# Two batches in two waves of 256 tokens instead of one after the other, at the start of a fused attention and FFN kernel

## The chip, the cores and the metric

The kernel runs on one core of a Trainium2 chip. The metric is device time in microseconds (us); 371.22 us is the median of three runs of the kernel before, which lie between 371.21 and 371.28. The span of a profile, from the first instruction to the last, is a little shorter than the time of the same execution.

## The reference

Block-causal attention over 8 batches, 8 heads, 576 tokens and a head dimension of 64, then a gated FFN on all 4608 tokens of 512 features:

```python
def _attn_ref(q, k, v):                      # [8, 8, 576, 64] each, f32
    scores = scale * np.matmul(q, k.transpose(0, 1, 3, 2))
    mask = (pos[:, None] // 64) >= (pos[None, :] // 64)     # blocks of 64
    scores = np.where(mask, scores, -1000000000.0)
    ...                                      # softmax over the last axis
    return np.matmul(attn, v)

x = attn_out.transpose(0, 2, 1, 3).reshape(B * S, H * D)    # [4608, 512]
gate = np.maximum(x @ w_gate, 0.0)           # w_gate, w_val: [512, 1536]
out = (gate * (x @ w_val)) @ w_out           # w_out: [1536, 512]
```

## The kernel before, in words

Matmuls run in bf16, with sums in f32. The first 512 tokens of a batch are an *FFN tile*; the last 64 tokens of all eight batches (the *tails*) form the ninth. Heads are handled in pairs, `hp`, and `r = 4 * b + hp` numbers the 32 pairs of all batches.

For a pair, `scores` (matmul L418) computes scores transposed, keys on the partitions, in blocks of 128 tokens. Its two heads lie on partitions 0 to 63 and 64 to 127, so that their matmuls use two halves of the array. `exp` (L428, ScalarE, ACT) writes exponentials to `attnT[r % 2]`. A 128 by 128 block on the diagonal has one 64 by 64 corner that the mask forbids; `corners` (L498, L499) sets it to zero. `head_av` (L564) multiplies by v with a column of ones beside it, so that column 64 holds the sum. `normalise` (L511, L512, VectorE, DVE) divides and writes `xnat`, which `to_xT_pe` (L609) transposes on TensorE (PE) into `xT`, copied out of PSUM at L613 to L616. With 512 tokens a head has 10 blocks of scores at or below the diagonal.

q, k and v of the first batches come through `Early`: a DMA from the SP queue into an f32 tile `stage` (10 buffers), a cast to bf16 on POOL (GpSimd; L215 for q and k, L245 for v), then transposes on PE (`pe_mains`, L313) with copies out of PSUM (L316) into `qTm` and `kTm`. q and k have four consecutive tokens on a partition, so that a run of DRAM is 1 KB; the copies put them back in order. In batch 0, v is loaded with one token on a partition (`load_v`, runs of 256 bytes) and cast straight to `v_bf` (L231). In batch 1, v is loaded packed like q and k, cast to `v_p`, and brought into order by matmuls with a 0/1 matrix `sel` (`sort_v`, L263), in four groups of 32 rows, with the copies at L272.

The FFN is a generator, `ffn_gen`. An FFN *unit* is one of 12 columns of 128 hidden features: four matmuls for the gate and four for the value (L656), a Relu on ACT (L665) and a product on DVE to `hT` (L669). Then come four output blocks of 12 matmuls each (L677), copied at L687 and stored. `ffn(n)` lets it run on by n matmuls, to the end of a unit or block. PSUM has 8 banks: `take(1)` and `pair()` hand out banks 0 to 5, those taken longest ago first; banks 6 and 7 (`AV`) are for attention times v.

Every engine runs its instructions in the order in which the code issues them. The order at the start is written by hand: batch 0's loads, casts and attention first, with the weights' loads and casts (L407) behind, then FFN tile 0, in which `ffn(...)` calls alternate with the attention of batch 1. The end of tile 0 also has the transposes (`pe_tails`, L336) and scores of the tails (`scores_last`, L470; `scores_tails`). Tile 1 needs `xT` of batch 1. Where a few matmuls (`junk`, L716) multiply zeros, they only keep PE busy.

Of the kernel before, what the change touches and what calls it, by code (L numbers as in the profile page):

```python
# [17 lines left out]
def kernel(  # L18
# [23 lines left out]

    consts = ctx.enter_context(tc.tile_pool(name="consts", bufs=1))
# [5 lines left out]
    AV = 6  # L49
# [33 lines left out]
    zeros = consts.tile([128, 512], BF, name="zeros")  # L83
    nc.vector.memset(zeros, 0.0)

    sel = consts.tile([128, 516], BF, name="sel")
# [13 lines left out]
    def selection(eng):  # L100
        eng.memset(sel, 0.0)
        for c in range(4):
            ps = slice(32 * c, 32 * c + 32)
            eng.tensor_copy(
                sel[ps].rearrange("p (j m) -> p j m", j=4)[:, :, 0:128:4],
                ident[ps, None, 32 * c : 32 * c + 32].to_broadcast([32, 4, 32]),
            )
# [35 lines left out]
    class Early:  # L143
# [10 lines left out]

        def load(self, st, src, h0, n, eng=None):
            (eng or nc.sync).dma_start(  # L156
                st.rearrange("p (h n) -> p h n", h=n),
                src[self.b, h0 : h0 + n, 0:512, :].rearrange(
                    "h (p j) d -> p h (j d)", j=4
                ),  # L160
            )
# [13 lines left out]

        def load_v(self, h0, n):
            st = self.st[2, h0] = new_stage(256 * n)
            for h in range(n):
                nc.sync.dma_start(
                    st[:, 256 * h : 256 * h + 256].rearrange("p (c d) -> p c d", c=4),  # L180
                    v[self.b, h0 + h, 0:512, :].rearrange("(c p) d -> p c d", p=128),
                )
# [47 lines left out]
        def cast_v(self, h0, n, eng):  # L230
            eng(  # L231
                v_bf[self.b % 2][:, 0:4, h0 : h0 + n, 0:64].rearrange(
                    "p c h d -> p h c d"
                ),
                self.st[2, h0].rearrange("p (h c d) -> p h c d", h=n, c=4),
            )

# [18 lines left out]
        def sort_v(self, h0, engs):  # L256


            tp = [pair() for _ in range(2)]
            for j in range(4):  # L260
                for c in range(4):
                    ps = slice(32 * c, 32 * c + 32)
                    nc.tensor.matmul(  # L263
                        tp[c // 2][:, c % 2, 0:256],
                        sel[ps, 128 * j : 128 * j + 128],
                        v_p[ps, j, 64 * h0 : 64 * h0 + 256],
                        start=(j == 0),
                        stop=(j == 3),
                        skip_group_check=True,
                    )  # L270
            for i in range(2):
                engs[i](  # L272
                    v_bf[self.b % 2][:, 2 * i : 2 * i + 2, h0 : h0 + 4, 0:64],
                    tp[i][:, :, 0:256].rearrange("p g (h d) -> p g h d", d=64),
                )
# [134 lines left out]
    def scores(b, hp, sc, pieces):  # L410
        for pos, c, main in pieces:
            for hh in range(2):
# [3 lines left out]
                if main:  # L416
# [3 lines left out]
                    kTm[b % 2][ps, c, hp, :],  # L420
# [9 lines left out]
    def scores_1(r):  # L430

        b, hp = divmod(r, 4)
        at = attnT[r % 2]
        sc = scores(b, hp, banks[:, 0:2] if r % 2 == 0 else banks[:, 2:4], [(0, 0, True)])
        exp(at[:, :, 0:512], sc)
        sc = scores(
            b, hp, banks[:, 2:4] if r % 2 == 0 else banks[:, 0:2],
            [(0, 1, True), (384, 3, True)],
        )
        exp(at[:, :, 512:1024], sc)  # L440

    def scores_2(r):
        b, hp = divmod(r, 4)
        sc = scores(b, hp, banks[:, 0:2] if r % 2 == 0 else banks[:, 2:4], [(0, 2, True)])
# [499 lines left out]
```

## Time and profile before

| | |
|---|---|
| median of the runs | 371.22 us |
| profiled execution: its time, its span | 371.53 us, 369.7 us |
| PE busy | 355.9 us, 96% of the span |
| DVE, ACT, POOL busy | 163.2, 172.3, 116.5 us |
| first scores on PE | 6.48 us from the span's start |
| first FFN matmul of tile 0 | 20.34 us |
| first FFN matmul of tile 1 | 66.41 us |
| granted TensorE clock | 1.0 throughout |

A timeline row gives the start, the time that it covers, the engine, line and operation, output and inputs with their shapes, a count, and in brackets the idle time ahead of it on that engine with what ended it. PEld is the loading of weights into the array, which overlaps PE. SPq and ACTq rows are the issues of DMAs. Matmuls overlap each other, so PE's step from one group to the next is the difference of their starts, not the time of a row.

### The profile page before, as it was taken

How to read it: one execution, taken by the hardware profiler on the slowest of the kernel's cores; microseconds unless marked ns; L12 is line 12 of the kernel's file. 1: busy time of each engine (PE TensorE's matmuls, PEld its weight loads, DVE VectorE, ACT ScalarE, POOL GpSimd, SP SyncE). 2: the span in 40 equal slices, each digit the busy share in tenths (PEclk: the TensorE clock that was granted, in tenths of full speed). 3: DMA queues.
4: the chain of work that ended last, by engine and by line, in shares of the span. 5: the costliest groups of instructions: out<-in, count | busy, mean ns of one | idle time of the engine just before them, and what ended most of it. 6: DMA issues, size and time to landing. Idle time of an engine off the chain costs nothing.

```text
span 369.7 us, 7494 instructions
## 1 busy us (share of the span) xinstructions
PE 355.9 (96%) x2961; PEld 187.3 (51%) x3000; DVE 163.2 (44%) x319; ACT 172.3 (47%) x271; POOL 116.5 (31%) x163
## 2 busy tenths in 40 slices
PE   6799899999999999999999999999999999999995
PEld 3545356555555555555555555555555544444443
DVE  4634345376375543444434443444344434423422
ACT  5934656756574563465435543644364403302310
POOL 8677775156778404900391013000000000000000
PEclk9999999999999999999999999999999999999999
DMA  8999989779999979997499829072200130020013
GB/s 255 291 370 355 376 181 328 153 177 256 196 164 167 153 126 94 181 82 151 82 181 92 139 76 136 19 140 68 92 16 18 47 101 0 2 85 29 2 42 100
DMA packets 140227, 51.02 MB, mean 138 GB/s; under 512 B 119584, under 2 KB 133152, under 8 KB 140192
## 3 DMA queue, kind: packets, MB, share of 16 engines
q1 hardware_dynamic: 78528, 34.29, 39.8%
q0 software_dynamic: 56384, 7.08, 35.8%
q10 hardware_dynamic: 5280, 9.18, 7.0%
q8 instruction: 23, 0.38, 0.5%
q14 instruction: 12, 0.10, 0.1%
HBM read 37.75 MB, written 9.44 MB: 128 GB/s over the span
## 4 chain that ended last, share of the span: by engine, by line
PE 85%; DMA 9%; DVE 1%; ACT 1%; issue 1%; POOL 1%; SPq 1%; DVEq 0%; POOLq 0%
PE banks L656 46%; PE banks L677 24%; PE banks L564 7%; PE banks L418 6%; DMA stage<-in_moe_w_gate_dram 3%; DMA stage<-in_v_dram 2%; DMA qTt<-q_bt 2%; DMA stage<-in_k_dram 1%; PE banks L530 1%; SPq L156 1%; ACT attnT L428 0%; DVE hT L669 0%; ACT xT L616 0%; PE banks L609 0%; POOL v_p L245 0%
## 5 line engine op out<-in xcount | busy, mean ns | idle before, releaser
L428 ACT ACTIVATE attnT<-banks 128x1024 bf16<-128x1024 f32 (+1 forms) x124 | 89.8, 811 | 60.4 <-PE banks L418 59.7
L665 ACT ACTIVATE gate_sb<-banks 128x512 bf16<-128x512 f32 x108 | 65.2, 603 | 100.9 <-PE banks L656 100.6
L669 DVE TENSOR_TENSOR hT<-gate_sb,banks 128x512 bf16<-128x512 bf16 x108 | 74.2, 687 | 83.7 <-PE banks L656 74.1
L656 PE MATMUL banks<-xT,wg 128*128 128x512 bf16 x366 | 98.0, 379 | 1.0
L656 PE MATMUL banks<-xT,wv 128*128 128x512 bf16 x378 | 98.4, 379 | 0.3
L677 PE MATMUL banks<-wo,hT 128*128 128x512 bf16 (+1 forms) x432 | 96.1, 373 | 0.6
L656 PEld LDWEIGHTS <-wv 128*128 128x128 bf16 x432 | 42.3, 98 | 51.0
L677 PEld LDWEIGHTS <-hT 128*128 128x128 bf16 x444 | 42.3, 98 | 46.1
L656 PEld LDWEIGHTS <-wg 128*128 128x128 bf16 x432 | 40.4, 98 | 45.9 <-issue 0.8
L687 DVE COPY ob<-banks 128x512 f32<-128x512 f32 (+1 forms) x37 | 25.1, 677 | 54.0 <-PE banks L677 53.2
L361 POOL DMA_DIRECT2D v_bf<-in_v_dram x16 | 14.1, 901 | 70.1 <-PE banks L564 68.1
L564 PE MATMUL banks<-v_bf,attnT 128*128 128x65 bf16 x832 | 35.1, 194 | 1.0 <-POOL v_bf L231 0.6
L564 PEld LDWEIGHTS <-attnT 128*128 128x128 bf16 x832 | 30.6, 98 | 9.7 <-issue 1.6
L418 PE MATMUL banks<-qTm,kTm 64*128 64x512 bf16 (+3 forms) x256 | 25.0, 298 | 2.4 <-ACT attnT L428 1.4
L512 DVE TENSOR_TENSOR xnat<-banks,recip 128x640 bf16<-128x640 f32 (+2 forms) x36 | 25.9, 721 | 1.2
L418 PEld LDWEIGHTS <-kTm 64*128 64x128 bf16 x512 | 17.1, 94 | 12.4 <-issue 3.1
L511 DVE RECIPROCAL recip<-banks 128x10 f32<-128x10 f32 (+3 forms) x38 | 8.0, 210 | 30.3 <-PE banks L564 28.5
L498 DVE MEMSET attnT<- 64x192 uint32 x28 | 6.1, 218 | 23.1 <-ACT attnT L428 20.3
L361 POOL DMA_DIRECT2D q_bf<-in_q_dram x16 | 14.4, 941 | 0.0
L361 POOL DMA_DIRECT2D k_bf<-in_k_dram x16 | 14.2, 928 | 0.7 <-DMA v_bf<-in_v_dram 0.6
L656 PE MATMUL banks<-xTt,wg 128*128 128x512 bf16 x48 | 12.3, 379 | 0.1
L656 PE MATMUL banks<-xTt,wv 128*128 128x512 bf16 x46 | 12.1, 379 | 0.1
(90 smaller groups left out, 194.5 us busy)
## 6 DMA issues: line engine op xcount, KB each, us to landing
out_dram<-ob ACTq DMA_DIRECT2D x32, 256.0 KB, 2.3
stage<-in_moe_w_gate_dram SPq DMA_DIRECT2D x6, 512.0 KB, 9.4
stage<-in_moe_w_val_dram SPq DMA_DIRECT2D x6, 512.0 KB, 9.6
stage<-in_q_dram SPq DMA_DIRECT2D x6, 512.0 KB, 6.4
stage<-in_k_dram SPq DMA_DIRECT2D x6, 512.0 KB, 7.6
stage<-in_moe_w_out_dram SPq DMA_DIRECT2D x6, 512.0 KB, 9.0
stage<-in_v_dram SPq DMA_DIRECT2D x8, 256.0 KB, 6.4
q_bf<-in_q_dram POOLq DMA_DIRECT2D x16, 128.0 KB, 5.9
```

Source lines behind the costliest of these rows:

```text
L361: nc.gpsimd.dma_start(dst, src[b, :, 128 * c : 128 * c + n, :].rearrange("h p d -> p h d"),)
L418: nc.tensor.matmul(o, kTm[b % 2][ps, c, hp, :], qTm[b % 2][ps, c:4, hp, :] if main else qTt[b % 2][ps, hp, :], start=True, stop=True,)
L428: nc.scalar.activation(out, sc, AF.Exp, scale=scale)
L498: eng.memset(three[:, :, :, 0:64], 0.0)
L511: nc.vector.reciprocal(recip, av[:, :, :, 64])
L512: nc.vector.tensor_tensor(out=out, in0=av[:, :, :, 0:64], in1=recip.to_broadcast([rows, heads, n, 64]), op=AX.mult,)
L564: nc.tensor.matmul(av[:, 0, p, :], w, vb[:, c, h, :], start=(p == 0), stop=(c == p), skip_group_check=True,)
L656: nc.tensor.matmul(out[:, t, :], (wg, wv)[t][i][:, c, fo : fo + 128], x[:, c, :], start=(c == 0), stop=(c == 3),)
L665: nc.scalar.activation(gate_sb, out[:, 0, :], AF.Relu)
L669: nc.vector.tensor_tensor(out=h, in0=gate_sb, in1=out[:, 1, :], op=AX.mult)
L677: nc.tensor.matmul(op, hT[f][:, 128 * s : 128 * (s + 1)], wo[f // 4][:, f % 4, n0:n1], start=(f == 0), stop=(f == 11),)
L687: nc.vector.tensor_copy(ob, op)
```

## The change

`Early(0)` and `Early(1)` no longer stand for batches 0 and 1, but for two *waves*: wave 0 has tokens 0 to 255 of both batches, wave 1 tokens 256 to 511 of both. The first half of the partitions holds batch 0 and the second half batch 1. Each wave is an FFN tile, and the stores go to the rows that fit. Wave 0 needs 3 blocks of scores per head and batch (`scores_a`, `av_a`); wave 1 needs 7 (`scores_b`, `av_b`, once per pair and batch), with keys from both waves. Loads of q, k and v become two DMAs of 64 partitions each. v of wave 0 is packed and sorted by matmuls too; `sort_v` now uses two groups of 64 rows. The first FFN units of tiles 0 and 1 are merged, so that their matmuls go by the four head pairs: the last pair's `xT` is read by the last four of 16 matmuls.

```diff
+    def chunk(b, c):
+        return (c // 2, 2 * b + c % 2) if b < 2 else (b % 2, c)
...
+            self.parts = (
+                [(0, b, 0, 512)]
+                if b > 1
+                else [(64 * i, i, 256 * b, 256) for i in range(2)]
+            )
         def load(self, st, src, h0, n, eng=None):
+            for p0, b, s0, ns in self.parts:
+                (eng or nc.sync).dma_start(
+                    st[p0 : p0 + ns // 4].rearrange("p (h n) -> p h n", h=n),
+                    src[b, h0 : h0 + n, s0 : s0 + ns, :].rearrange(
+                        "h (p j) d -> p h (j d)", j=4
+                    ),
+                )
...
+        def sort_v(self, h0, engs, out=None):
+            out = pair() if out is None else out
+            for odd in range(2):
+                for j in range(4):
+                    for g in range(2):
+                        ps = slice(64 * g, 64 * g + 64)
+                        nc.tensor.matmul(
+                            out[:, g, 256 * odd : 256 * odd + 256],
+                            sel[ps, odd, 128 * j : 128 * j + 128],
+                            v_p[ps, j, 64 * h0 : 64 * h0 + 256],
...
+    def scores_a(hp):
+        at = wave_a(hp)
+        sc = banks[:, 0:2]
+        scores_wave(hp, sc, [(0, 0, 0, 0, 2), (256, 0, 2, 2, 2)])
+        exp(at[:, :, 0:512], sc)
+        sc = banks[:, 2:4]
+        scores_wave(hp, sc, [(0, 0, 1, 1, 1), (128, 0, 3, 3, 1)])
+        exp(at[:, :, 512:768], sc[:, :, 0:256])
...
+    def scores_b(hp, b):
+        at = attnT[b]
+        sc = pair()
+        scores_wave(hp, sc, [(256 * c, 0, 2 * b + c, 4 + 2 * b, 2) for c in range(2)])
+        exp(at[:, :, 0:512], sc)
+        sc = pair()
+        scores_wave(
+            hp, sc,
+            [(0, 1, 2 * b, 4 + 2 * b, 2), (256, 1, 2 * b + 1, 4 + 2 * b + 1, 1)],
+        )
+        exp(at[:, :, 512:896], sc[:, :, 0:384])
...
+            groups = [(0, 1)] if j < 2 else [(0,), (1,)]
+            groups += [(f,) for f in range(2, 12)]
...
-        for h0 in (2, 4, 6):
-            e0.load_qk(h0, 2)
-        for h0 in (0, 2, 4, 6):
-            e0.load_v(h0, 2)
+        e0.load_qk(2, 2, nc.scalar)
+        e0.load_v_packed(0)
+        e0.load_qk(4, 2)
+        e0.load_qk(6, 2)
+        e0.load_v_packed(4)
...
+        scores_a(0)
+        e0.pe_mains(1, (dve, dve), banks[:, 4:6])
+        scores_a(1)
+        e0.cast_qk(4, 2, (pool, pool))
+        corners_a(0, nc.gpsimd)
+        e0.sort_v(0, (dve, dve), banks[:, 6:8])
+        e0.cast_qk(6, 2, (pool, pool))
+        corners_a(1, nc.gpsimd)
+        e0.cast_v_packed(4, pool)
+        e0.pe_mains(2, (dve, act), banks[:, 4:6])
+        av_a(0, banks[:, 6:8])
+        scores_a(2)
+        corners_a(2, nc.gpsimd)
+        e0.pe_mains(3, (dve, dve), banks[:, 4:6])
+        av_a(1, banks[:, 6:8])
+        scores_a(3)
+        e0.sort_v(4, (act, dve), banks[:, 4:6])
+        corners_a(3, nc.vector)
         cast_w(w_0[0], pool)
+        to_xT_pe(0, (act,), banks[:, 0])
+        av_a(2, banks[:, 6:8])
+        to_xT_pe(1, (act,), banks[:, 1])
+        av_a(3, banks[:, 4:6])
         cast_w(w_0[1], pool)
+        to_xT_pe(2, (act,), banks[:, 2])
+        to_xT_pe(3, (act, dve), banks[:, 3])
...
+        ffn(40)
         e1.pe_mains(0, (dve, act))
         ffn(8)
+        scores_b(0, 0)
+        corners_b(0, nc.vector)
+        e1.pe_mains(1, (dve, act))
+        ffn(8)
+        scores_b(0, 1)
+        corners_b(1, nc.vector)
         e1.sort_v(0, (dve, act))
         ffn(8)
+        av_b(0, 0)
+        scores_b(1, 0)
+        corners_b(0, nc.vector)
+        av_b(0, 1)
+        wave_to_xnat(4, banks[:, AV : AV + 2])
+        scores_b(1, 1)
+        corners_b(1, nc.vector)
+        ffn(12)
...
+        scores_b(3, 0)
+        corners_b(0, nc.vector)
+        av_b(2, 1)
+        wave_to_xnat(6, banks[:, AV : AV + 2])
         e0.pe_tails((dve, act))
+        scores_b(3, 1)
+        corners_b(1, nc.vector)
+        e1.pe_tails((dve, act))
         to_xT_pe(6, (act,))
         scores_last(0)
+        av_b(3, 0)
+        scores_tails(0)
+        av_b(3, 1)
+        wave_to_xnat(7, banks[:, AV : AV + 2])
+        scores_last(1)
         to_xT_pe(7, (dve,))
```

POOL, from its first q cast on, in the kernel before (`v_bf` is written straight from `stage`):

```order
L215 CAST q_bf<-stage 128x2x4x64
L215 CAST k_bf<-stage 128x2x4x64
L215 CAST q_bf<-stage 128x2x4x64
L215 CAST k_bf<-stage 128x2x4x64
L215 CAST q_bf<-stage 128x2x4x64
L215 CAST k_bf<-stage 128x2x4x64
L498 MEMSET attnT_91 64x2x3x64
L499 MEMSET attnT_91 64x2x64
L231 CAST v_bf_93<-stage 128x2x4x64
```

and the same place after the change, where `v_p` is the packed v:

```order
L223 CAST q_bf<-stage 128x2x4x64
L223 CAST k_bf<-stage 128x2x4x64
L245 CAST v_p<-stage 128x4x4x64
L223 CAST q_bf<-stage 128x2x4x64
L223 CAST k_bf<-stage 128x2x4x64
L462 MEMSET attnT_91 64x2x3x64
L463 MEMSET attnT_91 64x2x64
L223 CAST q_bf<-stage 128x2x4x64
L223 CAST k_bf<-stage 128x2x4x64
```

The cast of v for heads 0 to 3 has moved ahead of q and k of heads 4 to 7, and the zeroing of the first pair's corners ahead of heads 6 and 7.

DVE at the end of tile 0 before (`ob` is an output block, L512 normalises the last pair, `qTt` are the tails' q of the two batches):

```order
L687 COPY ob<-banks 128x512
L511 RECIPROCAL recip<-banks 128x2x4
L512 TENSOR_TENSOR xnat<-banks,recip 128x2x4x64
L337 COPY qTt_83<-banks 128x256
L337 COPY qTt_84<-banks 128x256
L616 COPY xT<-banks 128x512
```

and after (L480 is `corners_b`, which can only run when the exponentials of its batch and pair are written; L583 normalises):

```order
L752 COPY ob<-banks 128x512
L480 MEMSET attnT_91 64x2x2x32
L582 RECIPROCAL recip<-banks 128x2x4
L583 TENSOR_TENSOR xnat<-banks,recip 128x2x4x64
L338 COPY qTt_83<-banks 128x256
L480 MEMSET attnT_92 64x2x2x32
L338 COPY qTt_84<-banks 128x256
L582 RECIPROCAL recip<-banks 128x2x4
L583 TENSOR_TENSOR xnat<-banks,recip 128x2x4x64
L675 COPY xT<-banks 128x512
```

Two zeroings and one more normalisation now stand between the last output block and the last copy to `xT`.

More of the change, by code (lines that the diff above doesn't have):

```diff
@@ L254, in cast_v_tail @@
                 eng(v_diag(self.b % 2, hh), self.st["t", 2][64 * hh : 64 * hh + 64])
[L256 to L270, printed above, removed]
+        def sort_v(self, h0, engs, out=None):
[8 more added lines that the diff above has]
+                            v_p[ps, j, 64 * h0 : 64 * h0 + 256],
+                            start=(j == 0 and odd == 0),
+                            stop=(j == 3),
+                            skip_group_check=True,
+                        )
             for i in range(2):
@@ new lines, in av_b @@
+    def av_b(hp, b, heads=(0, 1)):
+        at = attnT[b]
+        for hh in heads:
+            av = banks[:, AV + hh, 0:260].rearrange("p (n d) -> p n d", d=65)
+            for i in range(2):
+                for c in range(3 + i):
+                    k_i, k_c = chunk(b, c)
+                    col = 768 if c == 3 else 256 * c + 128 * i
+                    nc.tensor.matmul(
+                        av[:, 2 * b + i, :],
+                        at[:, hh, col : col + 128],
+                        v_bf[k_i][:, k_c, 2 * hp + hh, :],
+                        start=(b == 0 and i == 0 and c == 0),
+                        stop=(c == 2 + i),
+                        skip_group_check=True,
+                    )
@@ L554, in head_av @@
         vb = v_bf[b % 2]
[L555 to L557 removed]
+        av = banks[:, AV + hh, 0:325].rearrange("p (n d) -> p n d", d=65)
+        for p in range(NCH):
             for c in range(p + 1):
```

243 lines of the change are left out of this document (104 added, 139 removed).

## The prediction

> **What bounds the kernel now.** I read the page first, then the stages, then TensorE (PE) in order of time over the first 66 us, then the engines that feed it there.
>
> ```profile
> span 369.7 us, 7494 instructions
> PE 355.9 (96%) x2961; PEld 187.3 (51%) x3000; DVE 163.2 (44%) x319; ACT 172.3 (47%) x271; POOL 116.5 (31%) x163
> 0.00:20.34 20.34, 15.16 (x176) 9.00 (x177) 11.12 (x33) 13.78 (x19) 15.32 (x40) 1.00 1.02 281
> 20.34:66.41 46.07, 43.40 (x385) 22.75 (x388) 20.02 (x41) 24.11 (x43) 30.94 (x36) 1.00 1.04 318
> ```
>
> PE is the bound: 13.8 us idle in all. The last two lines are stretches (length; busy time of PE, weight loads, DVE, ACT, POOL; granted clock, DMA share, GB/s): the start up to the first FFN matmul, and FFN tile 0 with the next attention woven in, up to the first matmul of tile 1. Behind 66.41 nothing but order of little weight changes, so whatever PE gains or loses up to that point stays. The profiled execution took 371.53 us, 1.83 more than its span; the median of the runs is 371.22, 0.31 lower. I make the sum on the profiled one.
>
> ```profile
> 6.48 0.61 PE L418 MATMUL banks<-qTm,kTm 64*128 64x512 bf16 x6 [0.25 <-ACT kTm L316]
> 20.34 0.81 PE L656 MATMUL banks<-xT,wg 128*128 128x512 bf16 x3
> 22.07 1.03 PE L656 MATMUL banks<-xT,wg 128*128 128x512 bf16 x4
> 23.79 1.03 PE L656 MATMUL banks<-xT,wg 128*128 128x512 bf16 x4
> 38.49 0.62 PE L263 MATMUL banks<-v_p,sel 32*128 32x256 bf16 x16 [1.55 <-POOL v_p L245]
> 39.04 1.04 PE L656 MATMUL banks<-xT,wg 128*128 128x512 bf16 x3
> 40.87 0.71 PE L418 MATMUL banks<-qTm,kTm 64*128 64x512 bf16 x7
> 41.79 0.27 PE L418 MATMUL banks<-qTm,kTm 64*128 64x256 bf16 x1 [0.20 <-DVE hT L669]
> 42.00 1.02 PE L656 MATMUL banks<-xT,wg 128*128 128x512 bf16 x4
> 46.46 0.27 PE L418 MATMUL banks<-qTm,kTm 64*128 64x256 bf16 x1 [0.20 <-DVE hT L669]
> 46.66 0.79 PE L564 MATMUL banks<-v_bf,attnT 128*128 128x65 bf16 x20
> 47.28 2.76 PE L677 MATMUL banks<-wo,hT 128*128 128x512 bf16 x11
> 49.88 0.33 PE L313 MATMUL banks<-ident,q_bf 128*128 128x128 bf16 x3
> 62.60 0.77 PE L564 MATMUL banks<-v_bf,attnT 128*128 128x65 bf16 x20
> 63.21 0.39 PE L609 MATMUL banks<-ident,xnat 128*128 128x128 bf16 x4
> 63.53 0.29 PE L336 MATMUL banks<-ident,q_bt 64*128 64x64 bf16 x4
> 63.98 0.39 PE L609 MATMUL banks<-ident,xnat 128*128 128x128 bf16 x4
> 66.41 0.82 PE L656 MATMUL banks<-xT,wg 128*128 128x512 bf16 x2
> ```
>
> From starts to starts: an FFN unit 1.72, an output block 2.60, a sort of packed v 0.55, scores of a head pair 0.93 without the 0.20 wait, a pair's 20 AV matmuls 0.62 (31 ns each). The one long wait is 1.55 for packed v.
>
> **The start.** The same 3 MB of q, k and v come first, but per head only 6 causal blocks of 128 by 128 stand before the FFN instead of 10, and 768 columns of exponentials instead of 1280. What feeds PE there:
>
> ```profile
> 0.75 0.50 ACTq L156 DMA_DIRECT2D stage<-in_k_dram  x1
> 1.29 1.28 ACT L215 ACT_TABLE_LOAD   x1 [1.29 <-PEq L928]
> 4.51 0.62 ACT L215 CAST k_bf<-stage 128x512 bf16<-128x512 f32 x1 [1.94 <-DMA stage<-in_k_dram]
> 6.91 4.85 ACT L428 ACTIVATE attnT<-banks 128x1024 bf16<-128x1024 f32 x6 [0.49 <-PE banks L418]
> 7.05 0.61 POOL L215 CAST q_bf<-stage 128x512 bf16<-128x512 f32 x1 [0.16 <-DMA stage<-in_q_dram]
> 9.35 0.61 POOL L215 CAST k_bf<-stage 128x512 bf16<-128x512 f32 x1 [0.21 <-DMA stage<-in_k_dram]
> 37.40 1.04 POOL L245 CAST v_p<-stage 128x1024 bf16<-128x1024 f32 x1 [0.45 <-DMA stage<-in_v_dram]
> 7.45 0.69 DVE L316 COPY qTm<-banks 128x512 bf16<-128x512 bf16 x1 [1.16 <-PE banks L313]
> 8.06 0.68 DVE L316 COPY kTm<-banks 128x512 bf16<-128x512 bf16 x1
> 49.01 0.21 DVE L511 RECIPROCAL recip<-banks 128x8 f32<-128x8 f32 x1
> 49.26 0.69 DVE L512 TENSOR_TENSOR xnat<-banks,recip 128x512 bf16<-128x512 f32 x1
> 10.00:11.00 1.00, 0.62 (x8) 0.44 (x6) 0.85 (x2) 1.00 (x2) 0.91 (x3) 1.00 1.37 218
> 17.00:18.00 1.00, 0.57 (x10) 0.43 (x9) 0.34 (x2) 1.00 (x3) 0.61 (x3) 1.00 1.14 357
> 49.00:50.00 1.00, 1.00 (x8) 0.52 (x7) 0.90 (x2) 0.00 (x0) 1.00 (x1) 1.00 1.18 160
> ```
>
> Landing: 1.31 MB were there at 7.05 and 2.10 MB at 9.35, so 0.342 MB/us. ACT gets four DMA issues of 0.5 instead of one, then its table load, then four small copies for the selection matrix (no row; the bounds are 0 and the 0.61 of 512 columns, I take 0.2 each): its k cast starts near 4.95 instead of 4.51, and the first scores at 6.75 instead of 6.48. From there, each step at the quoted rows: casts of q, k for pair 1 end at 7.4, their copies out of PSUM at 8.8, scores 1 from 8.85. Packed v (1.57 MB) lands at 7.8, is cast until 8.85, sorted on PE 9.3 to 10.3. DVE then has no pause: two copies of sorted v (to 11.65), q of pair 2 (12.25), normalising pair 0 (0.9, to 13.15), q and k of pair 3 (14.4), normalising pair 1 (15.3). Scores 3 wait for k of pair 3 (14.45); ACT ends their exponentials at 16.4 (2 steps, 1.55) and copies its part of the second sorted v until 16.95. Then AV of pair 2, normalising 2 (18.45) and 3 (19.35), transposes, FFN at **19.65**, the first twelve matmuls needing only pairs 0 to 2. That is 0.7 earlier than 20.34. The floor, DVE's 9.1 us of work laid end to end from 7.5 with the last transpose, is 17.0. POOL's first weight casts end near 17: not the bound. Dropping v's 256-byte runs (218 GB/s, where 357 is the rule a little later) makes weights land some 2 us earlier, but no FFN unit waits for a weight in the rows before, so it is worth nothing by itself. Of the selection matrix, POOL loses 2.6 us of work, but its first cast then waits for the landing near 6.2; the doubled memset goes to DVE in the 1.7 it idled before its q cast. The seven junk matmuls taken out lie in waits. The merged units let 12 matmuls (2.6 us) instead of 6 run ahead of the last transpose's copies, which need 0.8. w_1 in column halves is ready sooner for two units that didn't wait. All these are worth nothing; so are the three DMA issues more that SP makes ahead of the next batch's v, since PE reaches that sort 3 us later than v_p is ready.
>
> **Tile 0.** More attention now lies under it: per head 14 of the two batches' 20 blocks instead of 10.
> - Sorts: two row groups of 64 instead of four of 32, twice the streaming; 0.55 becomes about 0.98: +0.86 for two (bounds 0 and 1.1, a doubling). The two sorts at the start stand in that stage.
> - Scores: 8 calls with 896 columns instead of 4 with 1280. Scaled by columns, a call of 0.93 becomes 0.65, which I take: 5.2 against 3.6, +1.6 (bounds: 0.93 as before, +3.8; 0.47 for the bare streaming of half the columns and the drain, 0).
> - AV: 112 matmuls instead of 80, +1.0.
> - The wait of 1.55 goes: the sort comes two units later on PE (near 41.7), v_p is ready at 38.5 at the latest.
>
> Work +3.5. Next, waits. The two 0.20 waits for hT and those of the stretch from 62.60 to 66.41 are replaced: it is 3.81 long, and AV (0.61), two tail transposes (0.45 each), three transposes (0.22 to 0.32) and the tails' scores (0.7 at most) leave 0.9 of waiting at most. Taking PSUM pairs in the order the code takes them, and ACT and DVE strictly in order:
>
> ```profile
> 41.35 2.49 ACT L428 ACTIVATE attnT<-banks 128x512 bf16<-128x512 f32 x4 [0.58 <-PE banks L418]
> 44.01 0.22 DVE L498 MEMSET attnT<- 64x192 uint32 x1 [2.28 <-POOL wo L407]
> 50.08 0.69 DVE L687 COPY ob<-banks 128x512 f32<-128x512 f32 x1
> 65.80 0.68 PE L418 MATMUL banks<-qTt,kTm 64*128 64x64 bf16 x31 [0.33 <-ACT kTt L337]
> ```
>
> A call of scores gives ACT 1.8 us (1024 and 768 elements by the 4.85 of six), PE 0.65. So PE runs into the banks: pe_mains(1) behind hT 0.3, the unit behind it 0.15, the sort 0.25, the second scores of pair 1 0.1, the first output block 0.3, scores of pair 2 0.75 (q, k copies queued behind ob), AV 0.15: 2.0. At the end DVE's corner memset of pair 3 stands ahead of normalising pair 2 and of the qTt copy and waits for the exponentials; PE waits 0.45 in the second scores of pair 3, 1.1 for the bank of the tail transposes, 0.95 for normalising pair 3: 2.5. Together 4.5 for the 2.9 (1.55 + 0.4 + 0.9) that go: +1.6. The stretch becomes 46.07 + 3.5 + 1.6 = 51.2.
>
> **Tile 1.** Two merged units take the time of two. The tail normalising now queues behind two hT products, 0.45 more wait, and scores_last(1) lies earlier, -0.15: +0.3.
>
> Sum: -0.7 + 5.1 + 0.3 = +4.7. 371.53 becomes 376.25, the median **376.0**.
>
> **Rivals.**
> - *Half-partition loads are slow.* Each load is now two of 64 partitions. For it: 160 GB/s at 49 to 50, where the tails' loads of 64 partitions and 256-byte runs pass, against 218 for 128 partitions of the same runs. Against it: the row mixes loads, and the two halves follow each other in the queue. With 160/218 the rate falls from 0.342 to 0.25: packed v of heads 4 to 7 lands 3 us later (15.5), its sort moves from 15.0 to 17.0 and the FFN to 21.05, +1.4: 377.4. [...]
> - *The new waits are covered.* ACT is busy 24.11 of 46.07, so there is room on average. Then only work counts: -0.7 + 3.5 - 1.55 = +1.25: 372.5. Against it: ACT's work comes in pairs of calls.
> - *The start packs to DVE's floor.* If copies and normalising never wait, the FFN starts at 17.0: -3.3. With waits no larger than before, -3.3 + 1.95 = -1.35: 369.9, faster. It decides from a start before 17.6; with my waits no possible start would do. For it: ACT's exponentials alone need only 6 us (four times 1.45). Against: the sorts on PE wait for landings, which leave DVE idle from 8.8 to 10.3.
> - *Nothing measurable*: a start near 18.4 with covered waits.
>
> **Numbers.** My forecast 0.55 (its own range 374.2 to 377.2); slow halves 0.13; covered waits 0.13; faster 0.09; no change 0.10. Faster and slower are counted from 0.2% (0.74 us, about what a measurement of this kernel can tell from no change). Leaving out the fast case, half of the no-change one and the slow halves' upper part, the range is 371.5 to 377.9. Faster 0.09, same 0.10, slower 0.81.
>
> **What would show it.** First L720 matmul of tile 0 near 19.65 (17 for the floor, 21 for slow halves); its first of tile 1 near 70.9 instead of 66.41; no PE wait for v_p; PE waits for ACT and DVE of about 4.5 us between them; sorts of about 1 us. It is wrong if scores_b takes much less than 0.65, or if PE's waits at the end of tile 0 stay under 1 us.

## The result, and the profile after

The changed kernel takes 385.23 us (median of four runs, 384.94 to 386.06) against 371.25 for the kernel before beside it: 1.0375 times as long, with an interval of 1.0354 to 1.0396. The forecast was slower, by 4.7 us; it is slower by 14.0, outside the range. Executions in a slower state (one of e8's four took 1607.55 us, one of the kernel before 419.51) are left out of every ratio below.

The page of the changed kernel and its two stretches, cut as before: up to the first FFN matmul, and from there to the first of tile 1.

```profile
span 384.3 us, 7613 instructions
PE 362.3 (94%) x3018; PEld 192.4 (50%) x3057; DVE 163.6 (43%) x316; ACT 174.7 (45%) x272; POOL 114.9 (30%) x153
0.00:22.80 22.80, 15.00 (x170) 9.11 (x171) 11.58 (x29) 13.26 (x20) 11.70 (x29) 1.00 0.99 240
22.80:81.08 58.28, 50.38 (x453) 27.80 (x457) 20.51 (x41) 29.17 (x44) 31.32 (x36) 0.94 1.00 264
```

The start is 2.46 us longer, tile 0's stretch 12.21 (58.28 against 46.07), and what follows is the same (303.2 against 303.3): together the 14.6 of the spans. Look at the last two columns. The DMA engines are about as busy as before (0.99 and 1.00, against 1.02 and 1.04), but move 240 and 264 GB/s instead of 281 and 318. Both kernels move 20 to 21 MB up to tile 1 (length times rate), so the same data come later.

PE in order of time: start, time covered, count, and in brackets the idle time ahead with what ended it.

```profile
8.87 0.82 PE L441 MATMUL banks<-qTm,kTm 64*128 64x256 bf16 x8
18.41 1.05 PE L264 MATMUL banks<-v_p,sel 64*128 64x256 bf16 x16 [0.73 <-POOL v_p L245]
22.80 0.81 PE L720 MATMUL banks<-xT,wg 128*128 128x512 bf16 x2
40.89 0.40 PE L314 MATMUL banks<-ident,k_bf 128*128 128x128 bf16 x4 [1.85 <-POOL k_bf L223]
58.18 0.59 PE L742 MATMUL banks<-wo,hT 128*128 128x512 bf16 x2 [1.83 <-POOL wo L408]
75.92 0.34 PE L337 MATMUL banks<-ident,q_bt 64*128 64x64 bf16 x4 [1.07 <-DVE qTt L338]
80.85 0.40 PE L668 MATMUL banks<-ident,xnat 128*128 128x128 bf16 x4 [0.91 <-DVE xnat L583]
81.08 0.81 PE L720 MATMUL banks<-xT,wg 128*128 128x512 bf16 x2
```

The waits at 75.92 and 80.85 were forecast (1.1 and 0.95). Those at 40.89 and 58.18 were not: POOL's casts of k and of wo are late. What POOL waits for, in the changed kernel, and then its third weight cast and its last cast of wo in the kernel before:

```profile
17.32 1.04 POOL L245 CAST v_p<-stage 128x1024 bf16<-128x1024 f32 x1 [1.24 <-DMA stage<-in_v_dram]
22.84 1.04 POOL L408 CAST wg<-stage 128x1024 bf16<-128x1024 f32 x1 [1.69 <-DMA stage<-in_moe_w_gate_dram]
46.75 1.04 POOL L245 CAST v_p<-stage 128x1024 bf16<-128x1024 f32 x1 [1.55 <-DMA stage<-in_v_dram]
57.09 1.04 POOL L408 CAST wo<-stage 128x1024 bf16<-128x1024 f32 x1 [1.38 <-DMA stage<-in_moe_w_out_dram]
```

```profile
20.00 1.04 POOL L407 CAST wg<-stage 128x1024 bf16<-128x1024 f32 x1 [0.24 <-DMA stage<-in_moe_w_gate_dram]
45.55 1.04 POOL L407 CAST wo<-stage 128x1024 bf16<-128x1024 f32 x1 [0.33 <-DMA stage<-in_moe_w_out_dram]
```

The third weight cast comes 2.84 us later than in the kernel before, the first cast of `v_p` in tile 0 9.35 us later (37.40 there), and the last of wo's six casts 11.5. Single microseconds of the two kernels, the last column GB/s: first the kernel before, then the changed one, while q and k of the first and of the second group of loads pass.

```profile
7.00:8.00 1.00, 0.65 (x14) 0.56 (x10) 0.55 (x1) 1.00 (x2) 0.85 (x2) 1.00 1.05 358
35.00:36.00 1.00, 1.00 (x6) 0.49 (x5) 0.71 (x2) 0.66 (x2) 0.63 (x2) 1.00 1.08 380
```

```profile
7.00:8.00 1.00, 0.53 (x5) 0.53 (x6) 0.45 (x1) 0.42 (x1) 0.00 (x0) 1.00 1.14 218
35.00:36.00 1.00, 1.00 (x7) 0.43 (x5) 0.69 (x1) 0.05 (x1) 0.89 (x1) 1.00 1.08 225
42.00:43.00 1.00, 1.00 (x4) 0.32 (x3) 0.00 (x0) 0.57 (x1) 0.61 (x1) 0.50 1.09 209
```

With loads of 64 partitions the rate is 0.6 of what it was (218 against 358 and 225 against 380 GB/s). q, k and v of a wave are 3.15 MB: at 218 to 225 GB/s some 14.2 us, at 358 to 380 some 8.5. That is 5.7 us more. Wave 0 makes the weights only 2.84 late, which fits that the kernel before brings its first v slowly too (218 GB/s at 10 to 11 us, in the prediction's rows). The rest is added behind it: from 32 to 38, 40 to 43 and 52 to 58 us, between the issue and the landing of wave 1's halves, every microsecond shows 159 to 239 GB/s. The last row also shows a granted clock of 0.50; it stood lowered from 41 to 46 and from 76 to 80 us.

### The profile page after: what moved, and what is told of

Its sections match the earlier page's. It is cut to its first block, busy times and chain, and to the rows that moved or that the text cites. A ratio compares the mean times of both kernels' runs of the same rounds, so it can differ in the third digit from the quotient of the medians.

```text
span 384.3 us, 7613 instructions
## 1 busy us (share of the span) xinstructions
PE 362.3 (94%) x3018; PEld 192.4 (50%) x3057; DVE 163.6 (43%) x316; ACT 174.7 (45%) x272; POOL 114.9 (30%) x153
## 4 chain that ended last, share of the span: by engine, by line
PE 81%; DMA 12%; issue 1%; SPq 1%; DVE 1%; ACT 1%; POOL 1%; POOLq 0%; ACTq 0%
PE banks L720 43%; PE banks L742 24%; PE banks L634 6%; DMA stage<-in_moe_w_val_dram 6%; PE banks L420 5%; DMA stage<-in_moe_w_out_dram 3%; DMA stage<-in_v_dram 3%; SPq L172 1%; PE banks L508 1%; PE banks L264 1%; PE banks L602 1%; PE banks L668 1%; DVE xnat L583 0%; DVE ob L752 0%; POOL v_p L245 0%
## 5 line engine op out<-in xcount | busy, mean ns | idle before, releaser
L720 PE MATMUL banks<-xT,wg 128*128 128x512 bf16 x366 | 99.6, 380 | 1.3 <-ACT v_p L430 0.2
L720 PE MATMUL banks<-xT,wv 128*128 128x512 bf16 x377 | 100.4, 382 | 0.3
L720 PEld LDWEIGHTS <-wv 128*128 128x128 bf16 x432 | 42.4, 98 | 51.2 <-issue 0.8
L634 PE MATMUL banks<-v_bf,attnT 128*128 128x65 bf16 x672 | 28.4, 194 | 0.0
L634 PEld LDWEIGHTS <-attnT 128*128 128x128 bf16 x672 | 24.8, 98 | 6.6
L583 DVE TENSOR_TENSOR xnat<-banks,recip 128x640 bf16<-128x640 f32 (+1 forms) x32 | 25.3, 791 | 1.1
L582 DVE RECIPROCAL recip<-banks 128x10 f32<-128x10 f32 (+2 forms) x34 | 7.4, 217 | 30.3 <-PE banks L634 25.3
L420 PE MATMUL banks<-qTm,kTm 64*128 64x512 bf16 (+1 forms) x192 | 17.4, 298 | 0.0
L420 PEld LDWEIGHTS <-kTm 64*128 64x128 bf16 x448 | 14.2, 96 | 5.9
L572 DVE MEMSET attnT<- 64x192 uint32 x24 | 5.2, 218 | 17.2 <-ACT attnT L430 16.6
L223 POOL CAST q_bf<-stage 128x1024 bf16<-128x1024 f32 (+1 forms) x9 | 9.2, 1022 | 10.6 <-DMA stage<-in_q_dram 10.4
```

Of the source, the lines that this page charges most:

```text
L223: engs[t](self.half(t, h0 // 4)[:, :, lo : lo + 64 * n].rearrange("p j (h d) -> p h j d", d=64), self.st[t, h0].rearrange("p (h j d) -> p ...
L420: nc.tensor.matmul(o, kTm[i][ps, ci, hp, :], qTm[b % 2][ps, c:4, hp, :] if main else qTt[b % 2][ps, hp, :], start=True, stop=True,)
L582: nc.vector.reciprocal(recip, av[:, :, :, 64])
L583: nc.vector.tensor_tensor(out=out, in0=av[:, :, :, 0:64], in1=recip.to_broadcast([rows, heads, n, 64]), op=AX.mult,)
L634: nc.tensor.matmul(av[:, p, :], w, vb[:, c, h, :], start=(p == 0), stop=(c == p), skip_group_check=True,)
L720: nc.tensor.matmul(out[f][:, t, :], (wg, wv)[t][i][:, c, fo : fo + 128], x[:, c, :], start=(c == 0), stop=(c == 3),)
```

## Experiments

**Which part of the change costs the time?** Three kernels. e2 is the kernel before with q, k and the packed v of batches 0 and 1 each loaded as two DMAs of 64 partitions:

```diff
-                st.rearrange("p (h n) -> p h n", h=n),
...
+            ks = 2 if self.b < 2 else 1
+            w = 128 // ks
+            for i in range(ks):
...
+                    st[w * i : w * i + w].rearrange("p (h n) -> p h n", h=n),
```

> The kernel before, with only the loads of q, k and packed v of batches 0 and 1 split into two DMAs of 64 partitions each; it computes what the reference does. 'Halves': 2 MB of q and k before the FFN move at about 230 GB/s instead of 350, later loads likewise; the first FFN matmul comes 1 to 3 us later than 20.34, the wait for packed v grows from 1.55 to 4 or 5, and the time rises by 4 to 8, to 375 to 379. 'Many small DMAs' predicts a rise as well, of 1 to 8, told apart by the run with full partitions. 'Work and bank waits': no rise beyond 1, 371 to 372.

Measured: 383.3 us against 371.68, ratio 1.0332 (1.0288 to 1.0377). The halves alone cost 11.6 us, more than was expected of them: the first FFN matmul comes at 24.84, and the wait for packed v grows from 1.55 to 4.01. That wait, and two of its microseconds:

```profile
46.85 1.04 PE L266 MATMUL banks<-v_p,sel 32*128 32x256 bf16 x16 [4.01 <-POOL v_p L248]
5.00:6.00 1.00, 0.14 (x1) 0.00 (x0) 0.20 (x1) 0.69 (x1) 0.51 (x2) 1.00 1.07 238
9.00:10.00 1.00, 1.00 (x12) 0.77 (x8) 0.12 (x1) 1.00 (x2) 0.64 (x2) 0.50 0.60 174
```

The DMA engines are reported full at 5 to 6 us (1.07) and yet move 238 GB/s; at 9 to 10 they are not even full (0.60). There SP's issues, one behind the other, are likely what sets the rate: two of 128 KB each take 1.30 us, or 202 GB/s, and the four microseconds from 7 to 11 show 198.5 in the mean. The granted clock of the profiled execution was lowered at times (0.50 in the second row), but it is not the main price: executions at a mean of 0.996 and 0.977 took 382.79 and 382.84 us.

e3 is the change with each wave's two batches on all 128 partitions (two tokens of each batch on a partition, runs of 512 bytes), so that a sort takes 8 matmuls:

```diff
-                    st[p0 : p0 + ns // 4].rearrange("p (h n) -> p h n", h=n),
+                    st.rearrange("p (h b n) -> p h b n", h=n, b=2)[:, :, b],
...
-                        "h (p j) d -> p h (j d)", j=4
+                        "h (p j) d -> p h (j d)", j=2
```

> The changed kernel with another layout of the waves: each batch on all 128 partitions, two consecutive tokens on a partition (runs of 512 bytes), the two batches beside each other in the free dimension; the sort of v then takes 8 matmuls of 64 rows instead of 16. It computes what the reference does. 'Halves': loads run at 280 to 350 GB/s, the first FFN matmul near 19.5 us, sorts of about 0.5 instead of 1.0 us, no wait for a cast of k or wo: about 375 (373.5 to 377). 'Many small DMAs': 383 to 385. 'Work and bank waits': 380 to 382.

Measured: 377.7 against 371.68, ratio 1.016 (1.0134 to 1.0185): 6.0 slower, a little above the expected range, and 8 us better than the change. No wait for k or wo is left in its tile 0, the first FFN matmul comes at 20.68, and that of tile 1 at 72.92.

e4 is the kernel before with batch 0's v packed and sorted in two groups of 64 (`load_v_packed` for `load_v`), without the waves:

```diff
-        for h0 in (0, 2, 4, 6):
-            e0.load_v(h0, 2)
+        e0.load_v_packed(0)
+        e0.load_v_packed(4)
...
+            if r == 0:
+                e0.cast_v_packed(0, pool)
+                e0.sort_v(0, (dve, act), banks[:, 6:8])
```

> The kernel before with one part of the change alone: v of batch 0 packed (runs of 1 KB, all partitions) and sorted by matmuls in two groups of 64 rows, also for batch 1; no waves, no merged units. It computes what the reference does. The 256-byte runs of v go, so weights and packed v of batch 1 land about 1.9 us earlier and the wait of 1.55 for it goes; against that two sorts of 1.0 instead of 0.55 under tile 0 (+0.9), and two sorts with their copies at the start, which put the first FFN matmul 0 to 1.5 us later than 20.34. 'Halves' and 'work and bank waits' expect 370 to 372; 'many small DMAs' (fewer here) the same or less.

Measured: 376.25, ratio 1.0129 (1.0112 to 1.0146), where no loss was expected. The one line that decides it:

```profile
11.96 1.80 PE L264 MATMUL banks<-v_p,sel 64*128 64x256 bf16 x16 [3.78 <-POOL v_p L245]
```

I had put the sort ahead of transposes that could have run, so PE stood 3.78 us for v. This prices my placing, not the change's, and settles nothing.

**Loads in full, the rest untouched.** e1 gives the change loads of 128 partitions and half the heads each. It reads tokens 0 to 511 of one batch instead of the waves' tokens.

```diff
+            k = len(self.parts)
+            m = n // k
+            for i in range(k):
...
-                    st[p0 : p0 + ns // 4].rearrange("p (h n) -> p h n", h=n),
-                    src[b, h0 : h0 + n, s0 : s0 + ns, :].rearrange(
+                    st.rearrange("p (h n) -> p h n", h=n)[:, m * i : m * i + m],
+                    src[self.b, h0 + m * i : h0 + m * i + m, 0:512, :].rearrange(
```

> The changed kernel with each load of q, k and v of the first two waves made by two DMAs of all 128 partitions and half the heads each, so that count, size and run length (1 KB) stay; the tokens that they bring are those of batch 0 or 1 alone, so the data are not those of the waves. Theory 'halves' (a transfer to 64 partitions is slow, the late loads stall PE and its idling lowers the granted clock): the rate in the first 17 us rises from about 230 to 350 GB/s, the first FFN matmul comes near 19.7 us instead of 22.8, PE waits for no cast of k or wo, the clock stays at 1, and the time is about 376 (374.5 to 377.5). Rival 'many small DMAs': nothing changes, 384 to 386. Rival 'work and bank waits under tile 0': the start gains 2 to 3, the rest stays, 381 to 383.

Measured: 383.76, ratio 1.0322 (1.0293 to 1.0352), only 1.5 better than the change. Taken by itself this spoke against the halves, but its profile does not:

```profile
7.00:8.00 1.00, 1.00 (x6) 0.45 (x5) 0.00 (x0) 0.46 (x1) 0.75 (x2) 1.00 1.01 321
```

With as many DMAs of the same size the loads run at 321 GB/s where the change has 218, so the count of DMAs alone does not make the change's rate. In tile 0 PE waits for no cast of k or wo, and tile 1 begins at 77.12 instead of 81.08 (in the fastest of four executions, 382.14, against the slowest of the change's, 386.06). The first FFN matmul stays at 22.87. Two more kernels looked for a second bound at the start. e6 is the change with the selection matrices copied by POOL instead of ACT, e9 does the same to e1:

```diff
-        selection(nc.vector.memset, nc.scalar.copy)
+        selection(nc.vector.memset, nc.gpsimd.tensor_copy)
```

> The change, with the four copies that build the selection matrices on GpSimd (as before) in place of ScalarE. If ScalarE's start (table load 1.28 us, four copies of 0.48 us, k's cast only at 6.80) sets the first FFN matmul: it goes from 22.80 to about 21.5 us, and the time to 384.0. Rival, by the landing rate of the half-partition loads: the casts of batch q2 (8.20), of v_p (10.52 and 17.32) wait for their DMAs as before, the sort at 18.41 stays where it is, the first FFN matmul stays within 0.5 us of 22.8, time 384.8 to 385.3.

> Both cures of the start at once: loads on all 128 partitions (as e1, which reads other tokens than the waves need) and the selection matrices copied on GpSimd (as e6). Each alone left the first FFN matmul where it was (22.87 and 22.79 against 22.80). If two chains of about the same length end there, ScalarE's and the landing of the halves: now it comes at 21.0 to 21.5, time 381.5 to 382.5. Rival, neither is the bound of the start, but the chain of transposes, evacuations on DVE and exp: still 22.5 or later, time 383.5.

e6: 385.42, ratio 1.0366 (1.0343 to 1.0388), first FFN matmul at 22.79: nothing, as the rival said. e9: first FFN matmul at 21.32, as expected of two bounds, but 384.09, ratio 1.0311 (1.0264 to 1.0358), 2 us above the expectation. The two bounds at the start are real: in the changed kernel ACT's four DMA issues, table load and four copies end only at 6.77, and the second v lands only at 17.3.

```profile
1.51 1.95 ACTq L172 DMA_DIRECT2D stage<-in_k_dram  x3
3.55 1.28 ACT L113 ACT_TABLE_LOAD   x1 [3.55 <-DVE sel L110]
4.84 1.93 ACT L113 COPY sel<-ident 32x128 bf16<-32x128 bf16 x4
6.80 0.62 ACT L223 CAST k_bf<-stage 128x512 bf16<-128x512 f32 x1
```

Where did e9 lose the gain again? Its ACT and PE near the end of tile 0:

```profile
68.88 0.34 ACTq L698 DMA_DIRECT2D out_dram<-ob  x1
69.32 1.73 ACT L432 ACTIVATE attnT<-banks 128x1024 bf16<-128x1024 f32 x2 [4.97 <-DMA stage<-in_v_dram]
```

```profile
70.39 0.39 PE L443 MATMUL banks<-qTm,kTm 64*128 64x256 bf16 x4 [3.61 <-ACT attnT L432]
```

An output store in ACT's queue is issued at 68.88, and ACT's wait of 4.97 ahead of the exponentials behind it ends with the landing of a v load of batch 2, which neither needs for its data. PE pays 3.61 for it; in e1 it pays 1.47 at the same place. The changed kernel's ACT waits 2.04 us there, for PE, and PE 0.31. e14 is e9 with tile 0's stores issued by POOL:

```diff
-            nc.scalar.dma_start(out[r0 : r0 + 128, :], ob)
+            (nc.scalar if j else nc.gpsimd).dma_start(out[r0 : r0 + 128, :], ob)
```

> e9 (loads on all 128 partitions, of other tokens than the waves need; selection matrices from GpSimd) with tile 0's output stores issued by GpSimd instead of ScalarE. In e9 ScalarE's store at 68.88 us stood 4.97 us for the landing of a v load of batch 2, the exp behind it came late, and TensorE waited 3.61 us at 70.39 and then ran at half clock; in e1 the same place cost 1.47. If that is what ate the gain of e1 and e9: the first FFN matmul of tile 1 comes at about 73.5 to 74.5 instead of 78.1, time 377.5 to 379.5. Rival, the store is only where a general lateness shows: 382 or more.

Measured: 379.29 against 372.19, ratio 1.0176 (1.0124 to 1.0229). So the larger part of the gain of full loads had been eaten by that store. With it out of the way they bring the excess from 14.0 to 7.1. The change itself with its stores moved was not run; that the store costs nothing there is read from its profile alone. Tile 0 of e14:

```profile
22.71:73.96 51.25, 46.98 (x454) 26.14 (x458) 20.51 (x41) 28.69 (x44) 32.15 (x40) 1.00 1.01 287
```

It is 7.0 shorter than the change's 58.28, with the same three waits at its end (0.31, 1.07 and 0.91). The change's granted clock was lowered in two pieces of its tile 0, each 1.71 us short of full, which are at most 3.4 of the 7.0. The start of e14 gained nothing in this execution: the clock stood at 0.50 from 8 to 14 us.

**The rest of the forecast's waits.** e8 is e3 with the tail transposes ahead of a stretch of FFN units and the tail scores behind the last AV:

```diff
+        e0.pe_tails((dve, act))
+        ffn(4)
+        e1.pe_tails((dve, act))
+        ffn(8)
-        ffn(12)
...
-        scores_tails(0)
         av_b(3, 1)
         wave_to_xnat(7, banks[:, AV : AV + 2])
+        scores_tails(0)
```

> The interleaved form (e3), with the tail transposes of batches 0 and 1 issued ahead of the last-but-one stretch of FFN units and the tail scores of batch 0 behind the last AV, so that the two waits at the end of tile 0 (1.07 for qTt, 0.91 for the last normalise) have work over them. By the account 'waits plus the clock that follows them': the waits go (about -2.0) and the stretch at half clock at 67 to 71 us goes with them (-1.7): first FFN matmul of tile 1 at about 69.3 instead of 72.9, time 374.0 (373.3 to 374.8). Rival, waits alone: 375.8. Rival, exp and evacuations on ScalarE and DVE are the true bound there and the wait comes back under another name: 377.5.

Measured against 371.8: ratio 1.0177 (1.013 to 1.0224), no better than e3; the single runs took 376.57, 377.22 and 380.41 us, at mean granted clocks of 0.999, 0.995 and 0.991. The two waits went, others came (0.95 for the last-but-one normalise, 0.54 for a PSUM pair of the merged units).

e12 adds to e8 eleven matmuls on zeros in the start's waits, single units at the start of tile 1, and the transposes of pair 2 behind one AV call:

```diff
-            groups = [(0, 1)] if j < 2 else [(0,), (1,)]
+            groups = [(0, 1)] if j < 1 else [(0,), (1,)]
...
+        junk(4, banks[:, 7])
         scores_a(1)
...
```

> The interleaved form with the tail order of e8, the transposes of pair 2 behind one AV call, the first two FFN units of tile 1 unmerged, and 11 matmuls on zeros in the three waits of the start of over 0.4 us. e8 took 376.57, 377.22 and 380.41 us at mean granted clocks of 0.999, 0.995 and 0.991. If the spread is the granted clock's answer to waits: it now stays at 0.998 or above in every run, and the time is 375.3 (374.8 to 376.3), within 0.5 of what was forecast for the change. Rival, the clock falls regardless or the fillers delay the work that they stand before: 377 to 378.

Measured: 376.16 against 371.45, ratio 1.0126 (1.0085 to 1.0168). Its two stretches, and its longest wait in tile 0:

```profile
0.00:20.10 20.10, 15.71 (x164) 8.78 (x165) 11.32 (x29) 12.07 (x20) 11.55 (x29) 1.00 0.93 267
20.10:72.42 52.32, 47.51 (x443) 25.52 (x441) 20.43 (x41) 27.99 (x43) 31.28 (x36) 1.00 1.02 294
37.11 0.40 PE L325 MATMUL banks<-ident,k_bf 128*128 128x128 bf16 x4 [1.08 <-POOL k_bf L232]
```

The median is 4.7 us slower, the very figure of the forecast, but in part by luck: e12 has its loads on all partitions, sorts with half the matmuls, has fillers and no wait of 1.07 at the end of tile 0, and waits 1.08 for k instead. The profiled execution is its slowest, 378.3. e16 is the change with its halves kept and all the other cures of e12, and the copies of the selection matrices on POOL:

```diff
-        selection(nc.vector.memset, nc.scalar.copy)
+        selection(nc.vector.memset, nc.gpsimd.tensor_copy)
...
+        junk(4, banks[:, 7])
         scores_a(1)
...
+        e0.pe_tails((dve, act))
+        ffn(4)
+        e1.pe_tails((dve, act))
+        ffn(8)
```

> The change with its half-partition loads kept, and every other cure of e12: selection matrices from GpSimd, the tail order, the fillers at the start, first two units of tile 1 unmerged. e12 took 376.16 with the interleaved loads, the change 385.23. If the landing of the halves is the larger part of the nine: 382.5 to 384 here, TensorE again waiting 1.5 us or more for k's and wo's casts at 40 to 60 us. Rival, the waits at start and end of tile 0 are the larger part: 379 to 381.

Measured: 385.2 against 372.19, ratio 1.0344 (1.0301 to 1.0388). In sum the cures bring nothing while the halves stay:

```profile
57.60 0.59 PE L742 MATMUL banks<-wo,hT 128*128 128x512 bf16 x2 [1.89 <-POOL wo L408]
```

Its profile reaches tile 1 at 79.09, 2.0 earlier than the change's, starts the FFN more than 1 us later (24.14 is its first recorded matmul), and takes 1.2 longer behind. So of the change's 14.0, the halves with their landing make about 7 (14.0 to 7.1 in e14), 8.3 between e16 and e12, of which the shorter sorts may be 2.0 (four sorts of 8 matmuls instead of 16, so half of 0.98 each).

**Are the halves slow because they follow each other in one queue?** e13 is the kernel before with batch 0's q and k in halves, one half from SP's queue, the other from ACT's (of the first k both are from ACT's):

```diff
-            (eng or nc.sync).dma_start(
-                st.rearrange("p (h n) -> p h n", h=n),
...
+            ks = 2 if self.b < 1 else 1
+            w = 128 // ks
+            for i in range(ks):
+                ((eng or nc.sync), nc.scalar)[i].dma_start(
+                    st[w * i : w * i + w].rearrange("p (h n) -> p h n", h=n),
```

> Before, with batch 0's q and k loaded as two halves of 64 partitions, the first half from SP's queue, the second from ScalarE's. e2 with both halves from SP moved 174 to 246 GB/s at 5 to 14 us, before 305 to 366 at 5 to 8 us. [...] Rival, packets of halves are slow whatever runs beside: under 250. The time itself says little, since ScalarE's issues delay its casts: 373 to 380.

```profile
5.00:6.00 1.00, 0.56 (x5) 0.30 (x3) 0.40 (x1) 0.00 (x0) 0.62 (x2) 1.00 1.04 257
6.00:7.00 1.00, 0.00 (x0) 0.00 (x0) 0.29 (x1) 0.00 (x0) 0.00 (x0) 1.00 1.04 304
```

Measured once, 375.31 us. From 4 to 8 us the mean of the four single microseconds is 276 GB/s, against 230 in e2 and 347 in the kernel before. Two queues bring back part of the rate: more than the 250 below which the rival put it, and 71 less than the kernel before. Why the rest is missing stays open.

**Is the 1.55 us wait a loss that the kernel before could save?** e5 is the kernel before with that sort two FFN units later; e10 also moves the transposes of pairs 2 and 3 one output block later:

```diff
         e1.pe_mains(1, (act, act))
-        e1.sort_v(0, (dve, act))
         ffn(8)
         scores_all(4, False)
         corners(4, nc.vector)
-        ffn(16)
+        ffn(8)
+        e1.sort_v(0, (dve, act))
+        ffn(8)
...
-        ffn(12)
+        ffn(16)
         e1.pe_mains(2, (dve, act))
         e1.pe_mains(3, (act, dve))
         to_xT_pe(4, (act,))
-        ffn(12)
+        ffn(8)
```

The first half is e5, both are e10.

> Before, with batch 1's first sort of packed v moved two FFN units later on TensorE, nothing else. If the 1.55 us that TensorE stands at 46 us for the v_p cast is a pure loss: the stretch from the first FFN matmul of tile 0 to that of tile 1 shrinks from 46.07 to about 44.6 us and the time to 369.7 (369.4 to 370.2). Rival: the sort lands beside the scores and its evacuations hold up DVE or ACT, a wait of the same size stands one or two units later: 371.2.

> Before, with the first sort of batch 1's v moved as in e5, and the transposes of pairs 2 and 3 of batch 1 one further FFN group later. In e5 the wait of 1.55 us for v_p turned into one of 1.23 us for k's cast, the next cast in the same queue. If the landing of the loads (every GpSimd cast from 20 to 52 us waits 0.3 to 1.1 us for its DMA) is what both wait for, this group of 2.6 us covers it and nothing else is late: stretch 44.9, time 370.2 (369.8 to 370.7). Rival, the debt moves on once more, to the second sort or the scores of pair 2: 371.4.

e5: ratio 0.9998 (0.9988 to 1.0007). The wait, which stands ahead of 38.49 in the kernel before and not at 46 as the expectation says, came back at the next cast in POOL's queue:

```profile
50.13 0.40 PE L313 MATMUL banks<-ident,k_bf 128*128 128x128 bf16 x4 [1.23 <-POOL k_bf L215]
```

e10: ratio 0.9992 (0.9971 to 1.0014). Both waits are gone from its profile and the stretch is 45.42 instead of 46.07, but its start ran at half clock from 11 to 15 us, and the median does not move. I found no version that beats the kernel before.

**The fillers.** e7 is the kernel before without the seven matmuls on zeros ahead of the FFN:

```diff
-        junk(5, banks[:, 0])
         to_xT_pe(3, (act, dve), banks[:, 4])
-        junk(2, banks[:, 1])
```

> Before, without the seven matmuls on zeros that fill TensorE's waits just ahead of the first FFN matmul (the change takes them away too). If an idle TensorE is answered by a lower granted clock: first FFN matmul still at 20.3 us, then some 3 to 4 us at a granted clock of 0.5, worth 1.7 us as in each such stretch of the changed kernel: 373.0 (372.6 to 373.5). Rival, no price on a short wait but the wait: clock 1.0 throughout, 371.3.

Measured: 372.7 against 371.8, ratio 1.0029 (1.001 to 1.0048). The wait that they covered shows (0.97 at 20.68), the first FFN matmul comes at 21.13, but the clock stays at 1.00 behind it. In the profiled run it fell elsewhere, from 11 to 16 us, after a wait of 0.98 for v at 11.42 that is 0.63 in the kernel before. Neither expectation holds: the removal costs some 0.9 us, and not by a clock that falls at that place. How it costs them stays open: the profiled execution has its first matmul of tile 1 at 66.46 (66.41 before) and loses its 1.6 us (a span of 371.3 against 369.7) behind that.

## Why the prediction was wrong, step by step

- *"Landing: 0.342 MB/us"* is the step that failed. It was read from loads of 128 partitions and used for loads of 64, which ran at 0.21 to 0.25 (213 to 253 GB/s from 5 to 17 us). The rival had the right rate and the right loads, and the chance of 0.13 was too low: the one row of the trace that bore on it, 160 GB/s, leant its way.
- *The price of that rival* failed as well: it stopped at the first FFN matmul (+1.4), and wave 1's halves had no price at all. *"No FFN unit waits for a weight ... worth nothing by itself"* took a covered wait for slack. In the kernel before each POOL cast from 20 to 47 us waits 0.24 to 0.52 us for its DMA, so lateness of one load passes undiminished to all that follow, and wave 1's adds to wave 0's. In the prediction's sum wave 1's loads add nothing; measured, `v_p`, which was to be ready at 38.5 at the latest, is cast from 46.75 on, and PE has new waits of 1.85 for k and 1.83 for wo.
- *"The wait of 1.55 goes"*: the wait for v_p went from that place, but e5 shows that it was not the sort's own. It was the lateness of the whole row of loads, which the next reader pays.
- *The start, -0.7*, came out as +2.46. ACT's copies took 0.48 each and not 0.2; a row for them existed, 2.07 us for four on POOL. The halves' DMAs took SP 0.62 us each to issue. The k cast came at 6.80 instead of 4.95. e1, e6 and e9 show that this and the landing both had to go before the start moved (22.87, 22.79, 21.32). In e8, whose interleaved loads need copies of 0.2 each only and whose sorts take half the matmuls, the first FFN matmul comes at 19.63, the 19.65 of the forecast; that this is luck in part shows in e3, which has the same start and came at 20.68.
- *Work +3.5*: sorts 0.96 where 0.98 was taken, 14 AV matmuls 0.42 to 0.53 where 0.43 was, but `scores_b` 0.49 from start to start, where nothing interrupts it, and not 0.65: eight of them are 3.9 us, hardly above the four of 0.93 before, where +1.6 was counted. The prediction had named this as a sign of being wrong. In e14 PE's busy time of the stretch is still 3.6 above that of the kernel before (46.98 against 43.40): right in sum, though the parts named here make only some 2.3 of it; what the rest is stays open.
- *Waits of 4.5 for the 2.9 that go*: at the end of tile 0 0.31, 1.07 and 0.91, where 0.45, 1.1 and 0.95 were worked out; the PSUM waits of under 0.4 in the stretch come to 1.25 instead of 2.0. Right in kind and nearly in size; in e14 PE's idle time of the stretch is 4.27 against 2.67 before, the +1.6 of the sum.
- *Tile 1, +0.3*: the stretch behind 81.08 is 0.1 shorter. Too small to matter.

By the spans the forecast lacked 7.1 us in tile 0 (12.21 where 5.1 was) and 3.2 in the start. Tile 0 as forecast, 51.2, is what e14 measures with full loads, 51.25, so its account of PE, ACT and DVE there was sound in sum, and what it lacked came with the landing of the halves; the granted clock (below) explains at most a part, since e16 at 0.999 is as slow as the change. In the start the halves and ACT's copies acted together; with both gone e9 is at 21.32, still 1.7 behind the 19.65.

## What to carry to other kernels

When a change alters the shape of a transfer, price the new shape on every transfer that takes it, and follow the lateness down the queue until some engine has real idle time in which to catch up; casts that each wait a little for their DMA (here 0.24 to 0.52 us) mean that there is none. A wait that moves to the next reader when its first reader is moved belongs to the supply, not to the reader. Where two bounds end at the same place, undoing one shows nothing: undo both before the first is acquitted.

## What the runs showed of the hardware

- In the changed kernel loads of 64 partitions, each with its other half behind it in the queue, moved 0.6 of the rate that loads of 128 had in the kernel before (218 against 358 GB/s at 7 to 8 us), with the DMA engines reported full (1.14).
- In the changed kernel's tile 0 the granted clock fell to 0.50 twice: the single microseconds from 41 to 46 show 0.92, 0.50, 0.50, 0.50, 0.87, those from 75 to 80 show 0.99, 0.50, 0.50, 0.50, 0.80, each time together 1.71 us short of full, or 3.4 us at 0.50. Such a piece followed waits of 1.85 (40.89) and 1.07 us (75.92), but none followed that of 1.83 (58.18), nor one of 5.10 us in e13 (PE idle up to 10.66 by the busy times of its single microseconds, all of which show 1.00 from 2 to 98 us). What sets it off these runs do not show.
- The granted clock of a row does not show all of PE's rate. In the changed kernel four transposes take 0.40 us from start to start at 9.62 and 0.23 at 15.40, at a granted clock of 1.00 both times.
- A lower mean clock cost little in kernels with late loads: e16 took 385.28 us at 0.999 and 386.49 at 0.980, e2 382.79 at 0.996 and 382.84 at 0.977 (but 386.45 at 0.976). That the supply is the bound there is the likely reason, not a shown one.
- ACT stood 4.97 us at a store whose wait ended, by the trace, with the landing of a load that it does not use (e9); with the store on POOL's queue the time fell from 384.09 to 379.29 (e14). Why the store waited for that load stays open.
